# Late F2 with traded banks and a seeded sum, and a transposed key-value product in small array tiles

## The chip, the cores and the metric

The kernel runs on one NeuronCore of a Trainium2 chip. The metric is the device time of one execution in microseconds (us). The kernel before takes 149.12 us, the median of 7 runs, which lie between 149.07 and 150.18.

The engines are TensorE (PE, matmuls, with PEld for the loads of the stationary operand), VectorE (DVE), ScalarE (ACT), GpSimd (POOL) and SyncE (SP, which issues nearly all transfers). Matmuls write to PSUM, eight banks of 512 fp32 columns. ACT and DVE take results out of PSUM.

## What is computed

x has 2048 tokens of 448 features. It is normalised once and feeds two branches, whose sum is added to x:

```
xn = layernorm(x)
# branch A: linear attention, 16 heads of 28
q, k, v = split(xn @ wqkv)
phi(u) = concat(softmax(u @ w_phi), softmax(-(u @ w_phi)))      # 56 features a head
kv  = phi(k)^T @ v            # 56 x 28 for each head, over all tokens
z   = sum over tokens of phi(k)
o   = (phi(q) @ kv) / (phi(q) @ z + 1e-6)
A   = concat(o) @ wo
# branch B: dense, 448 -> 1792 -> 448
B   = silu(xn @ w1) @ w2
out = x + A + B
```

All inputs and the output are bf16; products are summed in fp32.

## The kernel before

Tokens are cut in 16 tiles of 128, and in 4 chunks of 512 (c = 0 to 3). All matmuls come in pairs (`pair`, line 439): one half of the pair contracts over partitions 0 to 63 (LO), the other over 64 to 127 (HI), and each writes a bank of its own. So every matmul uses 64 rows and 128 columns of the array, and a pair runs side by side. PSUM's banks form four slots of two: slots 0 to 2 rotate (`take`, `give`), slot 3 (banks 6 and 7) is fixed.

The units of work, in the order that PE runs them:

- Chunk 0 is transposed and sent through F1 in pieces. Here the two halves of a pair trade banks from one phase to the next (`F1ph`, line 663), and `swapped` (line 638) makes PE wait for its own last matmul on a bank before the other half writes there.
- `F1` (line 683): hT = silu(w1^T xn^T), 7 blocks for a chunk, 7 pairs of 512 columns each; ACT evicts 1024 columns.
- `QK` (line 693): phi of q and k for one tile, with exponentials on ACT, sums on DVE and products on POOL; the q half goes through a DMA transpose into phT.
- `V` (line 719): v of two tiles. Each head has 29 columns in `vb`: 28 of v and a column of ones, which gives z.
- `KV` (line 733): for one tile, 8 pairs of matmuls. The stationary operand is phi(k) of two heads (128 columns with padding), the moving one is v of the same two heads (58 columns). LO and HI tokens sum into banks 6 and 7 over all 16 tiles. Only the two diagonal blocks of each product are used.
- `KVZ_fin` (line 740): after the last KV, ACT copies one bank's diagonal blocks, DVE adds the other's; even heads end up on partitions 0 to 55, odd ones on 64 to 119 of KVZ.
- `F2` (line 749): one tile of hT^T w2, 14 pairs of 448 columns. The two halves are two partial sums of the same tile in two banks. For tiles 0 to 7 (`F2_early`) ACT and DVE add them into Ye and POOL adds x. For tiles 8 to 15 (`F2_late`, line 772), ACT copies one bank to Yl, POOL adds x to it, and the other bank stays for WO.
- `U` (line 784): phi(q) @ kv of two tiles, 16 pairs of 29 columns; then den, reciprocal and four products on DVE, and a DMA transpose into oT.
- `WO` (line 810): two tiles of o @ wo, 7 pairs of 448 columns, each half for a tile of its own. For early tiles it starts its banks; for late ones it goes on in the F2 banks. DVE adds Ye or Yl, writes x_sb, and SP stores two tiles.

Order: chunks 0 to 2 interleave F1, QK, V, KV and early F2. In chunk 3, phase_e comes before F1. KV of the last tile follows F1's block 4, KVZ_fin comes behind it, and the first U stands inside block 6. The late part (lines 1056 to 1064) goes over k = 0 to 3: U of a late pair, F2_late of its two tiles, WO of an early pair and WO of the late pair.

PE's order is the order of the program. For the other engines, `schedule` (line 203) plans: a list scheduler places each operation by its estimated start and its due time, tries several passes and then shaken due times (`shaken=60`), and keeps the order with the shortest planned span. A wait is a semaphore for each operation that depends on another engine, so what stands behind it on its engine waits too.

Of the kernel before, what the change touches and what calls it, by code (L numbers as in the profile page):

```python
# [7 lines left out]
F32 = mybir.dt.float32  # L8
# [132 lines left out]
class _Prog:  # L141
# [58 lines left out]
            return 230.0  # L200
        return 110.0

    def schedule(self, pe0, passes=6, shaken=60):
        ops = self.ops
        for o in ops:
            for d in o.deps:
                ops[d].users.append(o.id)
            for d in o.odeps:
                assert ops[d].eng == o.eng, "order-only deps must be same-engine"
                ops[d].users.append(o.id)  # L210
        t = 0.0
        when = {}
        seen = False
        for o in ops:
            if o.eng == "pe":
                if o.name != "warm" and not seen:
                    seen = True
                    t = max(t, pe0)
                when[o.id] = t
                t += o.dur  # L220
        best = None
        base = when
        for k in range(passes + shaken):
            if k == passes:
                base = {oid: best[2][oid][0] for oid in best[1]["pe"]}
            order, span = self._pass(base, k - passes + 1)
            if best is None or span < best[0]:
                best = (span, order, [(o.start, o.end) for o in ops])
                if k >= passes:
                    base = {oid: ops[oid].start for oid in order["pe"]}  # L230
            if k < passes:
                base = {oid: ops[oid].start for oid in order["pe"]}
        for o, (a, b) in zip(ops, best[2]):
            o.start, o.end = a, b
        self.order = best[1]
        self.makespan = best[0]
        return best[1]
# [92 lines left out]
def bass_parallel_sum__linear_kernel_hedgehog__dense_activation_silu__prompt_kernel(  # L330
# [21 lines left out]
    with es:  # L352
        def sb(name, shape, dt):
            return es.enter_context(nc.sbuf_tensor(name, shape, dt))

        NE, NV, NX, NXC, NYE, NYL, NH = 6, 3, 4, 3, 8, 4, 3
        x_sb = sb("x_sb", [128, NT, D], BF16)
        xT_all = sb("xT", [128, NXC * NS * 512], BF16)
        w1_sb = sb("w1_sb", [128, NS, FH * 128], BF16)
# [8 lines left out]
        xnd = sb("xnd", [128, NX, NS * 128], BF16)  # L368
        Ye = sb("Ye", [128, NYE, D], F32)
        KVZ = sb("KVZ", [128, 8, DH + 1], BF16)  # L370
        KVt = sb("KVt", [128, 8, DH + 1], F32)
        BD = sb("BD", [128, NB, 2 * DH], BF16)
        ident = sb("ident", [128, 128], BF16)
        neghalf = sb("neghalf", [128, 1], F32)
# [11 lines left out]
        phT = ph_all[:].rearrange("p (t c n) -> p t c n", t=NT, c=8)  # L386
        wsrc = hT[:, NH - 1, FT - 1, :]
        ones_bf = wsrc[:, 0:128]
        CH = NS * 512
        Yl = xT_all[:].bitcast(F32)[:, CH:CH + NYL * D].rearrange("p (y n) -> p y n", y=NYL)  # L390
        NO = 4
        E_all = E[:].rearrange("p a b n -> p (a b n)")
        o_pr = E_all[:, 8192:8192 + NO * NS * 128].rearrange("p (b n) -> p b n", b=NO)
# [11 lines left out]
        def bank(b):  # L405
            return psum[:, b * 512:(b + 1) * 512]
# [325 lines left out]

        def KV(t):
            P.unit = f"KV{t}"
            for c in range(8):
                pair([(bank(6 + q)[:, c * 58:(c + 1) * 58], E[HALF[q], t % NE, 1, c * 128:(c + 1) * 128],
                       vb[HALF[q], (t // 2) % NV, t % 2, c * 58:(c + 1) * 58], t == 0 and c == 0, t == NT - 1)
                      for q in range(2)], 58, "kv")

        def KVZ_fin():  # L740
            P.unit = "KVZ"
            for q, (p0, p1) in enumerate(((0, 56), (64, 120))):
                v = [bank(6 + b)[p0:p1, 0:464].rearrange("p (c n) -> p c n", n=58)[:, :, q * 29:(q + 1) * 29] for b in range(2)]
                tmp = KVt[p0:p1]
                act(tmp, v[0], ACTF.Identity, 232, name="kvz_a")
                dst = KVZ[p0:p1]
                dve(lambda e, dst=dst, a=v[1], tmp=tmp: e.tensor_tensor(dst, a, tmp, ALU.add), d_dve(232), [v[1], tmp], [dst], "kvz_d")

        def F2(t, mid=None, at=7):
            c, j = divmod(t, 4)  # L750
# [15 lines left out]
            give(sl)  # L766
            pool(lambda e: e.tensor_tensor(y, y, x_sb[:, t, :], ALU.add), 1110, [y, x_sb[:, t, :]], [y], "ye_x")  # L767

        ylc = [0]
        ysl = {}  # L770

        def F2_late(t, mid=None, at=7):
            sl = F2(t, mid, at)
            y = Yl[:, ylc[0] % NYL, :]
            ylc[0] += 1
            q = 1 - (t % 2)
            b = bank(2 * sl + q)[:, 0:D]
            act(y, b, ACTF.Identity, D, name="yl")
            pool(lambda e: e.tensor_tensor(y, y, x_sb[:, t, :], ALU.add), 1110, [y, x_sb[:, t, :]], [y], "yl_x")  # L779
            ysl[t] = (sl, y)  # L780

        uc = [0]

        def U(t, sl=3):
            P.unit = f"U{t}"
            for i, tt in enumerate((t, t + 1)):
                for c in range(8):
                    o0 = i * 232 + c * 29
                    pair([(bank(2 * sl + q)[:, o0:o0 + 29], phT[q * 64:q * 64 + 56, tt, c, :], KVZ[q * 64:q * 64 + 56, c, :], True, True)
                          for q in range(2)], 29, "u", dur=25.0)  # L790
            ub = uc[0] % NO
            uc[0] += 1
            Uv = two(sl)[:, :, 0:464].rearrange("p b (c n) -> p b c n", n=29)
            dn = den[:, ub, :].rearrange("p (b c) -> p b c", b=2)
            dve(lambda e: e.tensor_scalar(dn, Uv[:, :, :, DH], EPS_DEN, None, ALU.add), 200, [Uv], [den[:, ub, :]], "den")
            dve(lambda e: e.reciprocal(rden[:, ub, :], den[:, ub, :]), 360, [den[:, ub, :]], [rden[:, ub, :]], "rden")
            for i in range(2):
                for q in range(2):
                    src = bank(2 * sl + q)[:, i * 232:(i + 1) * 232].rearrange("p (c n) -> p c n", n=29)[:, :, 0:DH]
                    src = src.rearrange("p c (s e) -> p c s e", e=4)  # L800
                    r = rden[:, ub, q * 16 + i * 8:q * 16 + (i + 1) * 8]
                    rb = r[:, :, None, None].broadcast_to([128, 8, NS, 4])
                    dst = o_pr[:, ub].rearrange("p (s n) -> p s n", s=NS)[:, :, i * 64:(i + 1) * 64].rearrange("p s (c r e) -> p c r s e", r=2, e=4)[:, :, q]
                    dve(lambda e, dst=dst, src=src, rb=rb: e.tensor_tensor(dst, src, rb, ALU.mult), d_dve(224),  # L804
                        [src, r], [dst], "o")
            P.dma(lambda e: e.dma_start_transpose(out=oT[:, ub], in_=o_pr[:, ub]), 0, reads=[o_pr[:, ub]],
                  writes=[oT[:, ub]], name="oT_dma", issue=1250.0, fixed=3100.0)
            return ub

        def WO(t, ub, sl, parts=((0, D),)):  # L810
            P.unit = f"WO{t}"
            late = t in ysl
            if late:
                s0, y0 = ysl[t]
                s1, y1 = ysl[t + 1]
            else:
                s0 = s1 = sl
                y0, y1 = (Ye[:, tt % NYE, :] for tt in (t, t + 1))
            bks = (2 * s0, 2 * s1 + 1)
            for a, b in parts:  # L820
                for s in range(NS):
                    pair([(bank(bks[q])[:, a:b], oT[HALF[q], ub, s, :], wo_sb[HALF[q], s, a:b],
                           (not late) and s == 0, s == NS - 1) for q in range(2)], b - a, "wo")
                for q, y in enumerate((y0, y1)):
                    bk = bank(bks[q])[:, a:b]
                    dst = x_sb[:, t + q, a:b]
                    dve(lambda e, bk=bk, y=y[:, a:b], dst=dst: e.tensor_tensor(dst, bk, y, ALU.add), d_dve(b - a),  # L827
                        [bk, y[:, a:b]], [dst], "out")
                P.dma(lambda e, a=a, b=b: e.dma_start(out=ov[:, t:t + 2, a:b], in_=x_sb[:, t:t + 2, a:b]),
                      service(2 * 128 * (b - a) * 2, 2 * (b - a)), reads=[x_sb[:, t:t + 2, a:b]], name="out_dma", out_slot=True)  # L830
            give(s0)
            if s1 != s0:
                give(s1)

        def FT_tr(b2):
            P.unit = "FT"
# [190 lines left out]

        ub = {}

        def first_u():  # L1030
            ub[EPAIRS[0]] = U(EPAIRS[0])

        LATE = list(range(8, 16))
        EPAIRS = [0, 2, 4, 6]
        for c in range(NCH):
            if c == NCH - 1:
                phase_e(c, F2E[c])
            if c > 0:
                for i in range(FH):
                    F1(c, i, first_u if c == NCH - 1 and i == 6 else None)  # L1040
                    if i in ((3, 4, 5, 6) if c == 1 else (1, 2, 4, 5) if c == 2 else (1, 2, 3, 4)):
                        kv(1)
                    if c == NCH - 1 and i == 4:
                        KVZ_fin()
# [8 lines left out]
                give(sl)  # L1053
            ub[t] = U(t, sl)

        for k in range(4):
            l0, e = LATE[2 * k], EPAIRS[k]
            if k:
                nextu(l0)
            F2_late(l0, None if k else (lambda: nextu(LATE[0], None)), 3)  # L1060
            F2_late(l0 + 1, (lambda: nextu(EPAIRS[k + 1])) if k + 1 < 4 else None)
            sl = take()
            WO(e, ub[e], sl)
            WO(l0, ub[l0], None)

        order = P.schedule(5500.0)
        ops = P.ops
# [105 lines left out]
```

The softmax here doesn't subtract the row's maximum and nothing guards it: scores larger than these inputs give would overflow.

## Time and profile before

| what | value |
|---|---|
| median of 7 runs | 149.12 us |
| the profiled execution | 149.75 us |
| its span | 147.86 us |
| PE busy | 141.8 us, 96% of the span |
| DVE busy | 96.3 us, 65% |
| ACT busy | 85.5 us, 58% |
| POOL busy | 84.5 us, 57% |
| granted clock of TensorE | 1.00 |
| KV on PE, 256 matmuls | 6.1 us busy |
| late F2 to the last matmul | 109.36 to 144.2 us |

Busy time counts the length of each instruction; matmuls overlap, and the length of each holds a modelled tail. What one costs in a full stream is read from the distance of the starts instead. The span runs from the first to the last instruction of the trace; the time of an execution has 1.89 us more around it.

### The profile page before, as it was taken

The numbers are of one execution on the slowest core, as the hardware profiler recorded it, in microseconds if no ns is written. First come the engines' busy times: TensorE is split into PE (matmuls) and PEld (weight loads), VectorE is DVE, ScalarE is ACT, GpSimd is POOL, SyncE is SP. The second block draws the span as 40 slices with busy tenths as digits, with TensorE's granted clock in tenths as the row PEclk, the third lists the DMA queues.
The fourth block names the chain that finished last, engine by engine and source line by source line (L and its number), as shares of the span: only waits on it lengthen the run. The fifth ranks groups of instructions, "written<-read, shape, count | busy, mean of one in ns | idle before, by whom it ended". The sixth has DMA issues, their size and how long they took to land.

```text
span 147.9 us, 4912 instructions
## 1 busy us (share of the span) xinstructions
PE 141.8 (96%) x2118; PEld 86.9 (59%) x2118; DVE 96.3 (65%) x182; ACT 85.5 (58%) x109; POOL 84.5 (57%) x95
## 2 busy tenths in 40 slices
PE   6999999999999999999999999999999999999990
PEld 2589875555555555555555556655566566666550
DVE  1867369999996496841067997871154884848533
ACT  4247779988667794975987758598571111011110
POOL 3335024149999959899122999999972204122230
PEclk9999999999999999999999999999999999999999
DMA  4998989964919982379760092333779244853323
GB/s 128 389 235 197 304 248 262 112 137 124 202 25 103 191 165 69 93 159 138 155 136 0 0 110 36 71 75 73 41 176 94 51 112 124 119 140 72 104 72 124
DMA packets 43709, 19.10 MB, mean 129 GB/s; under 512 B 36712, under 2 KB 43048, under 8 KB 43688
## 3 DMA queue, kind: packets, MB, share of 16 engines
q1 hardware_dynamic: 43032, 17.87, 60.5%
q10 hardware_dynamic: 656, 0.92, 1.8%
q8 instruction: 16, 0.26, 0.9%
q14 instruction: 5, 0.04, 0.1%
HBM read 8.17 MB, written 1.84 MB: 68 GB/s over the span
## 4 chain that ended last, share of the span: by engine, by line
PE 93%; DVE 2%; DMA 2%; issue 1%; DVEq 0%; ACT 0%
PE psum L448 92%; DMA x_sb<-in_A_x_dram 2%; PE psum L461 1%; DVE st L575 1%; DVE x_sb L827 0%; DVEq L1124 0%; DVE mv L579 0%; DVE ve L581 0%; ACT xT L466 0%; DVE xnd L598 0%; DVEq L1113 0%
## 5 line engine op out<-in xcount | busy, mean ns | idle before, releaser
L715 POOL TENSOR_TENSOR E<-E,Rk 128x896 bf16<-128x896 bf16 x32 | 53.3, 1698 | 7.1 <-DVE Rk L710 5.1
L448 PE MATMUL psum<-xT,w_sb 64*128 64x512 bf16 (+2 forms) x522 | 46.9, 323 | 0.2
L448 PE MATMUL psum<-w_sb,hT 64*128 64x448 bf16 x448 | 45.2, 349 | 0.0
L448 PEld LDWEIGHTS psum<-w_sb,hT 64*128 64x128 bf16 x448 | 24.1, 94 | 16.6
L708 DVE TENSOR_REDUCE Sk<-E 128x64 f32<-128x1792 bf16 x16 | 31.9, 2004 | 2.9 <-ACT E L466 2.9
L466 ACT ACTIVATE hT<-psum 128x1024 bf16<-128x1024 f32 (+1 forms) x29 | 28.0, 993 | 9.8 <-PE psum L448 9.6
L448 PEld LDWEIGHTS psum<-xT,w_sb 64*128 64x128 bf16 x522 | 25.2, 94 | 13.8 <-issue 0.4
L466 ACT ACTIVATE E<-psum 128x896 bf16<-128x896 f32 x32 | 27.4, 917 | 6.4 <-PE psum L448 5.2
L466 ACT ACTIVATE xT<-psum 128x448 f32<-128x448 f32 (+3 forms) x14 | 6.6, 475 | 31.7 <-PE psum L448 27.8
L448 PE MATMUL psum<-wqk,xT 64*128 64x448 bf16 x224 | 23.7, 349 | 0.0
L779 POOL TENSOR_TENSOR xT<-xT,x_sb 128x448 f32<-128x448 f32 x8 | 8.3, 1032 | 25.0 <-ACT xT L466 21.6
L448 PEld LDWEIGHTS psum<-wqk,xT 64*128 64x128 bf16 x224 | 12.2, 94 | 8.6
L583 POOL TENSOR_TENSOR rstd<-ve,neghalf 128x1 f32<-128x1 f32 x16 | 9.1, 570 | 7.4 <-DVE ve L581 6.6
L767 POOL TENSOR_TENSOR Ye<-Ye,x_sb 128x448 f32<-128x448 f32 x8 | 8.2, 1036 | 8.9 <-DVE Ye L765 8.9
L575 DVE BATCH_NORM_STATS2 st<-x_sb 128x6 f32<-128x448 bf16 x16 | 9.6, 603 | 3.9 <-DMA x_sb<-in_A_x_dram 3.9
L591 DVE TENSOR_SCALAR xnd<-x_sb,mv,rstd 128x896 bf16<-128x896 bf16 x12 | 8.3, 722 | 5.8 <-POOL rstd L583 5.7
L448 PE MATMUL psum<-wv_sb,xT 64*128 64x448 bf16 x112 | 12.0, 349 | 0.0
L765 DVE TENSOR_TENSOR Ye<-psum,Ye 128x448 f32<-128x448 f32 x8 | 5.0, 621 | 10.3 <-ACT Ye L466 10.3
L448 PE MATMUL psum<-wo_sb,E 64*128 64x448 bf16 x112 | 11.3, 349 | 0.0
L804 DVE TENSOR_TENSOR E<-psum,rden 128x224 bf16<-128x224 f32 x32 | 10.3, 383 | 0.4
L448 PEld LDWEIGHTS psum<-wo_sb,E 64*128 64x128 bf16 x112 | 6.2, 94 | 4.4
L448 PEld LDWEIGHTS psum<-wv_sb,xT 64*128 64x128 bf16 x112 | 5.9, 94 | 4.0
(47 smaller groups left out, 102.4 us busy)
## 6 DMA issues: line engine op xcount, KB each, us to landing
w_sb<-in_B_w_dram SPq DMA_DIRECT2D x4, 448.0 KB, 5.5
out_dram<-x_sb SPq DMA_DIRECT2D x8, 224.0 KB, 2.2
w_sb<-in_B_w_dram SPq DMA_DIRECT2D x4, 336.0 KB, 5.6
x_sb<-in_A_x_dram SPq DMA_DIRECT2D x2, 448.0 KB, 4.6
wv_sb<-in_A_wqkv_dram SPq DMA_DIRECT2D x2, 392.0 KB, 5.0
wo_sb<-in_A_wo_dram SPq DMA_DIRECT2D x14, 56.0 KB, 2.3
phT<-in_A_wqkv_dram SPq DMA_DIRECT2D x3, 224.0 KB, 3.5
w_sb<-in_B_w_dram ACTq DMA_DIRECT2D x1, 448.0 KB, 5.1
```

The source lines that it names most:

```text
L448: ins = e.matmul(dst, lhsT, rhs, start=st, stop=sp, skip_group_check=True)
L461: ins = e.transpose(dst, src, idn)
L466: return P.op("act", d_act(n), lambda e: e.activation(dst, src, func, scale=scale), reads=reads or [src], writes=writes or [dst], table=ta ...
L575: P.op("dve", 630, lambda e: e.bn_stats(st6[:, t, :], xs), [xs], [st6[:, t, :]], name="bnst", ordered=od)
L583: P.op("pool", 580, lambda e: e.tensor_tensor(rstd[:, t:t + 1], ve[:, t:t + 1], neghalf[:], ALU.pow), [ve[:, t:t + 1], neghalf[:]], [rstd[ ...
L591: dve(lambda e: e.tensor_scalar(dst, src, mv[:, t, 0:1], rstd[:, t:t + 1], ALU.subtract, ALU.mult), 734, [src, mv[:, t, 0:1], rstd[:, t:t ...
L708: dve(lambda e: e.tensor_reduce(Sk[:, t % 3, :].rearrange("p (h g) -> p h g", g=2), Er, AXL.X, ALU.add), d_dve(1792), [Er], [Sk[:, t % 3, ...
L715: pool(lambda e, Eh=Eh, Rb=Rb: e.tensor_tensor(Eh, Eh, Rb, ALU.mult), 1770, [Eh, Rh], [Eh], "phi%d" % qk)
L765: dve(lambda e: e.tensor_tensor(y, b, y, ALU.add), d_dve(D), [b, y], [y], "ye_d")
L767: pool(lambda e: e.tensor_tensor(y, y, x_sb[:, t, :], ALU.add), 1110, [y, x_sb[:, t, :]], [y], "ye_x")
L779: pool(lambda e: e.tensor_tensor(y, y, x_sb[:, t, :], ALU.add), 1110, [y, x_sb[:, t, :]], [y], "yl_x")
L804: dve(lambda e, dst=dst, src=src, rb=rb: e.tensor_tensor(dst, src, rb, ALU.mult), d_dve(224), [src, r], [dst], "o")
```

## The change

It has two parts.

1. Late F2 works on two tiles at once. In a first phase (`F2_ph(.., 0, ..)`) the LO half of the contraction goes to the first tile's bank and the HI half to the second tile's. In a second phase (1) the halves trade banks, so that each bank ends up with one tile's full sum. Before the first phase ACT writes x into both banks (`seed`), and no matmul clears them, so x is part of the sum, and WO of the pair goes on in the same banks. Nothing is left to add: ACT copies both banks to x_sb. Yl and POOL's additions are gone. U and WO are put between the phases. The last pair (14 and 15) is cut into column halves of 224, each in a slot of its own, with F2, WO, eviction (ACT for one bank, DVE for the other) and store by halves.
2. KV is transposed. v of one head (29 columns) is the stationary operand and phi(k) of the same head (64 columns) the moving one. Four heads share a bank on partitions 0, 32, 64 and 96, so that a matmul uses 64 rows and 32 columns of the array, and eight different tiles of the array follow one another. Only products of matching heads are made: 32 matmuls of 64 columns for a token tile, where 16 of 58 stood. At the end ACT and DVE add the two banks to KVb (in the space of xnd), two pairs of PE transposes (`KVZ_tr`) turn it, and ACT and DVE evict KVZ. KVZ_tr takes the first U's place inside F1's last block, and the first U moves into F2 of tile 8.

The first U matmul alone clears its bank now, and the planner shakes 160 times.

```diff
         def KV(t):
             P.unit = f"KV{t}"
-            for c in range(8):
-                pair([(bank(6 + q)[:, c * 58:(c + 1) * 58], E[HALF[q], t % NE, 1, c * 128:(c + 1) * 128],
-                       vb[HALF[q], (t // 2) % NV, t % 2, c * 58:(c + 1) * 58], t == 0 and c == 0, t == NT - 1)
-                      for q in range(2)], 58, "kv")
+            for a in range(4):
+                mms = []
+                for j in range(4):
+                    h = 2 * ((j // 2) * 4 + (a // 2) * 2 + j % 2) + a % 2
+                    for q in range(2):
+                        mms.append((bank(6 + q)[32 * j:32 * j + 29, a * 64:(a + 1) * 64],
+                                    vb[HALF[q], (t // 2) % NV, t % 2, h * 29:(h + 1) * 29],
+                                    E[HALF[q], t % NE, 1, h * 64:(h + 1) * 64], t == 0 and a == 0, t == NT - 1))
+                pair(mms, 64, "kv", dur=40.0)
...
+            v = [bank(6 + b)[:, 0:256] for b in range(2)]
+            act(KVt[:], v[0], ACTF.Identity, 256, name="kvz_a")
+            dve(lambda e: e.tensor_tensor(KVb, v[1], KVt[:], ALU.add), d_dve(256), [v[1], KVt[:]], [KVb], "kvz_d")
+
+        def KVZ_tr():
+            P.unit = "KVZ"
+            for b in range(2):
+                tpair([(bank16(6 + q)[:, b * 64:(b + 1) * 64], KVb[HALF[q], b * 128:(b + 1) * 128], ident[HALF[q], q * 64:(q + 1) * 64])
+                       for q in range(2)], 64, "kvz_tr")
...
+        def seed(t, sl, a, b):
+            P.unit = f"F2_{t}"
+            xs = [x_sb[:, t + q, a:b] for q in range(2)]
+            bk = [bank(2 * sl + q)[:, a:b] for q in range(2)]
+            for q in range(2):
+                act(bk[q], xs[q], ACTF.Identity, b - a, name="seed")
+
+        def F2_ph(t, sl, ph, a, b, mid={}):
+            c, j = divmod(t, 4)
+            for ft in range(FT):
+                P.unit = f"F2_{t + ph}"
+                mms = []
+                for q in range(2):
+                    h = q ^ ph
+                    mms.append((bank(2 * sl + h)[:, a:b], hT[HALF[q], c % NH, ft, (j + h) * 128:(j + h + 1) * 128],
+                                w2_sb[HALF[q], ft, a:b], False, False))
+                swapped(pair(mms, b - a, "f2"), (2 * sl, 2 * sl + 1), ph)
+                if ft in mid:
+                    mid[ft]()
...
+        def WO_two(t, ub, sl, a, b):
+            WO_mm(t, ub, sl, a, b, True)
+            for q in range(2):
+                bk = bank(2 * sl + q)[:, a:b]
+                dst = x_sb[:, t + q, a:b]
+                if q and b - a < D:
+                    dve(lambda e, bk=bk, dst=dst: e.tensor_copy(dst, bk), d_dve(b - a), [bk], [dst], "out")
+                else:
+                    act(dst, bk, ACTF.Identity, b - a, name="out")
+            store(t, a, b)
+            give(sl)
...
-                    F1(c, i, first_u if c == NCH - 1 and i == 6 else None)
+                    F1(c, i, KVZ_tr if c == NCH - 1 and i == 6 else None)
...
+        def ph0(l, a, b, mid={}):
+            sls[l, a] = take()
+            seed(l, sls[l, a], a, b)
+            F2_ph(l, sls[l, a], 0, a, b, mid)
+
+        def ph1(l, a, b):
+            F2_ph(l, sls[l, a], 1, a, b)
+
+        def wo2(e, l):
+            WO(e, ub[e])
+            nextu(l + 2)
+            WO_two(l, ub[l], sls[l, 0], 0, D)
+
+        M = D // 2
+        ph0(8, 0, D, {1: lambda: nextu(0), 4: lambda: nextu(8, None)})
+        nextu(2)
+        ph1(8, 0, D)
+        ph0(10, 0, D)
+        wo2(0, 8)
+        ph1(10, 0, D)
+        nextu(4)
+        ph0(12, 0, D)
+        wo2(2, 10)
+        ph1(12, 0, D)
+        nextu(6)
+        ph0(14, 0, M)
+        wo2(4, 12)
+        ph1(14, 0, M)
+        ph0(14, M, D)
+        WO(6, ub[6])
+        ph1(14, M, D)
+        WO_two(14, ub[14], sls[14, 0], 0, M)
+        WO_two(14, ub[14], sls[14, M], M, D)
```

More of the change, by code (lines that the diff above doesn't have):

```diff
@@ L201, in lat, with schedule @@
         return 110.0
-    def schedule(self, pe0, passes=6, shaken=60):
+    def schedule(self, pe0, passes=6, shaken=160):
         ops = self.ops
@@ L354, in sb @@
             return es.enter_context(nc.sbuf_tensor(name, shape, dt))
-        NE, NV, NX, NXC, NYE, NYL, NH = 6, 3, 4, 3, 8, 4, 3
+        NE, NV, NX, NXC, NYE, NH = 6, 3, 4, 3, 8, 3
         x_sb = sb("x_sb", [128, NT, D], BF16)
@@ L370, in bass_parallel_sum__linear_kernel_hedgehog__dense_activation_silu__prompt_kernel @@
         KVZ = sb("KVZ", [128, 8, DH + 1], BF16)
-        KVt = sb("KVt", [128, 8, DH + 1], F32)
+        KVt = sb("KVt", [128, 256], F32)
+        KVb = xnd[:, 0, 0:256]
         BD = sb("BD", [128, NB, 2 * DH], BF16)
@@ L388, in bass_parallel_sum__linear_kernel_hedgehog__dense_activation_silu__prompt_kernel @@
         ones_bf = wsrc[:, 0:128]
-        CH = NS * 512
-        Yl = xT_all[:].bitcast(F32)[:, CH:CH + NYL * D].rearrange("p (y n) -> p y n", y=NYL)
         NO = 4
@@ L734, in KV @@
             P.unit = f"KV{t}"
-            for c in range(8):
-                pair([(bank(6 + q)[:, c * 58:(c + 1) * 58], E[HALF[q], t % NE, 1, c * 128:(c + 1) * 128],
-                       vb[HALF[q], (t // 2) % NV, t % 2, c * 58:(c + 1) * 58], t == 0 and c == 0, t == NT - 1)
-                      for q in range(2)], 58, "kv")
+            for a in range(4):
[7 more added lines that the diff above has]
+                pair(mms, 64, "kv", dur=40.0)
         def KVZ_fin():
             P.unit = "KVZ"
[L742 to L747, printed above, removed]
+            v = [bank(6 + b)[:, 0:256] for b in range(2)]
[7 more added lines that the diff above has]
+            for q in range(2):
+                src = bank16(6 + q)[:, 0:128].rearrange("p (c n) -> p c n", n=32)[:, :, 0:29]
+                dst = KVZ[:, 4 * q:4 * q + 4, :]
+                if q:
+                    dve(lambda e, dst=dst, src=src: e.tensor_copy(dst, src), d_dve(116), [src], [dst], "kvz_e")
+                else:
+                    act(dst, src, ACTF.Identity, 116, name="kvz_e")
         def F2(t, mid=None, at=7):
@@ L767, in F2_early @@
             pool(lambda e: e.tensor_tensor(y, y, x_sb[:, t, :], ALU.add), 1110, [y, x_sb[:, t, :]], [y], "ye_x")
[L769 to L780, printed above, removed]
+        def seed(t, sl, a, b):
[16 more added lines that the diff above has]
+                    mid[ft]()
         uc = [0]
@@ L788, in U @@
                     o0 = i * 232 + c * 29
-                    pair([(bank(2 * sl + q)[:, o0:o0 + 29], phT[q * 64:q * 64 + 56, tt, c, :], KVZ[q * 64:q * 64 + 56, c, :], True, True)
+                    pair([(bank(2 * sl + q)[:, o0:o0 + 29], phT[q * 64:q * 64 + 56, tt, c, :], KVZ[q * 64:q * 64 + 56, c, :], i == 0 and c == 0, True)
                           for q in range(2)], 29, "u", dur=25.0)
@@ L808, in U, with store, WO_mm @@
             return ub
-        def WO(t, ub, sl, parts=((0, D),)):
+        def store(t, a, b):
+            P.dma(lambda e: e.dma_start(out=ov[:, t:t + 2, a:b], in_=x_sb[:, t:t + 2, a:b]),
+                  service(2 * 128 * (b - a) * 2, 2 * (b - a)), reads=[x_sb[:, t:t + 2, a:b]], name="out_dma", out_slot=True)
+        def WO_mm(t, ub, sl, a, b, seeded):
             P.unit = f"WO{t}"
[L812 to L833, printed above, removed]
@@ new lines, in WO_mm, with WO @@
+            for s in range(NS):
+                op = pair([(bank(2 * sl + q)[:, a:b], oT[HALF[q], ub, s, :], wo_sb[HALF[q], s, a:b], (not seeded) and s == 0, s == NS - 1)
+                           for q in range(2)], b - a, "wo")
+                swapped(op, (2 * sl, 2 * sl + 1), 0)
+        def WO(t, ub):
+            sl = take()
+            WO_mm(t, ub, sl, 0, D, False)
+            for q in range(2):
+                bk = bank(2 * sl + q)[:, 0:D]
+                y = Ye[:, (t + q) % NYE, :]
+                dst = x_sb[:, t + q, :]
+                dve(lambda e, bk=bk, y=y, dst=dst: e.tensor_tensor(dst, bk, y, ALU.add), d_dve(D), [bk, y], [dst], "out")
+            store(t, 0, D)
+            give(sl)
@@ L835, in FT_tr @@
+        def WO_two(t, ub, sl, a, b):
+            WO_mm(t, ub, sl, a, b, True)
+            for q in range(2):
+                bk = bank(2 * sl + q)[:, a:b]
+                dst = x_sb[:, t + q, a:b]
+                if q and b - a < D:
+                    dve(lambda e, bk=bk, dst=dst: e.tensor_copy(dst, bk), d_dve(b - a), [bk], [dst], "out")
+                else:
+                    act(dst, bk, ACTF.Identity, b - a, name="out")
+            store(t, a, b)
+            give(sl)
         def FT_tr(b2):
@@ L1028, in bass_parallel_sum__linear_kernel_hedgehog__dense_activation_silu__prompt_kernel @@
         ub = {}
-        def first_u():
-            ub[EPAIRS[0]] = U(EPAIRS[0])
         LATE = list(range(8, 16))
@@ L1054, in nextu @@
             ub[t] = U(t, sl)
[L1056 to L1064, printed above, removed]
+        sls = {}
+        def ph0(l, a, b, mid={}):
[28 more added lines that the diff above has]
+        WO_two(14, ub[14], sls[14, M], M, D)
         order = P.schedule(5500.0)
```

## The prediction

> **What bounds the kernel now.** I read the page first, then busy time by stage, the chain, the timeline of the switch from F1 to late F2, the timeline of the end, and groups kept apart by shape. The page's first part:
>
> ```profile
> PE 141.8 (96%) x2118; PEld 86.9 (59%) x2118; DVE 96.3 (65%) x182; ACT 85.5 (58%) x109; POOL 84.5 (57%) x95
> ```
>
> By stage (busy us of PE, PEld, DVE, ACT and POOL, then clock and DMA):
>
> ```profile
> 33.87:97.47 63.60, 63.60 (x810) 36.78 (x808) 44.90 (x58) 47.73 (x56) 52.43 (x47) 1.00 0.62 107
> 97.47:109.36 11.89, 11.89 (x196) 6.69 (x194) 4.12 (x7) 9.09 (x12) 11.89 (x9) 1.00 0.54 82
> 109.36:144.20 34.84, 34.80 (x562) 21.37 (x558) 21.97 (x60) 5.37 (x9) 8.89 (x9) 1.00 0.48 98
> 144.20:147.90 3.70, 0.00 (x0) 0.00 (x0) 1.16 (x2) 0.00 (x0) 0.00 (x0) 0.99 0.33 124
> ```
>
> PE is full in every stage up to 144.2 us, at full clock, and the chain (start, length, what) says the same:
>
> ```profile
> 20.48 123.70 PE psum L448 x1724
> 144.18 0.03 issue
> 144.20 0.02 DVEq L1113
> 144.22 0.04 issue
> 144.27 0.62 DVE x_sb L827
> 144.89 0.53 DVEq L1124
> ```
>
> So only two things move the time: what PE has to stream, with any new hole in it, and the 3.7 us after its last matmul. Work taken off ACT, DVE or POOL before 144.2 is worth nothing by itself. The end in the timeline:
>
> ```profile
> 141.34 2.82 PE L448 MATMUL psum<-wo_sb,E 64*128 64x448 bf16 x28
> 144.27 1.16 DVE L827 TENSOR_TENSOR x_sb<-psum,xT 128x448 bf16<-128x448 f32 x2 [0.24 <-PE psum L448]
> ```
>
> For small matmuls, the starts of neighbouring PE rows give the price (a row's own length includes about 0.16 us of modelled tail: 349 ns against 187 ns of streaming for 448 columns):
>
> ```profile
> 105.71 0.40 PE L448 MATMUL psum<-vb,E 64*128 64x58 bf16 x16
> 105.94 1.90 PE L448 MATMUL psum<-xT,w_sb 64*128 64x512 bf16 x16
> 107.66 0.57 PE L448 MATMUL psum<-KVZ,phT 56*128 56x29 bf16 x32
> 108.07 0.39 PE L448 MATMUL psum<-xT,w_sb 64*128 64x512 bf16 x2
> ```
>
> One token tile's KV takes 0.23 us (8 pairs, 29 ns a pair); one U takes 0.41 us (16 pairs, 25.6 ns a pair). Every tile shape in the trace is 64 rows by 128 columns.
>
> **The change, part by part.**
>
> *KV.* Per token tile, 16 matmuls of 58 columns become 32 of 64 columns, in four groups of eight; a group fills eight array tiles of 64x32. The lower bound of a group is the streaming of 64 columns: the 14 transposes of 64 columns at 11.25 us take 0.20 us, 29 ns a pair, so 4 x 29 = 0.117 us. The upper bound is U's sustained rate, 12.8 ns a matmul with its weight load: 32 x 12.8 = 0.41 us. Between them: two weight loads of 94 ns each finish within 0.10 us at 8.67 us (row below), so instructions for different tiles can start about 5 ns apart; eight give 40 ns a group, 0.16 us a tile. I take this, because both U's and KV's rates are those of one tile used again, and here eight are in turn. Against 0.23 that is 16 x 0.07 = -1.12 us (bounds -1.81 and +2.88).
>
> *Change of tile shape.* KV stands in 14 blocks between 128-column matmuls (12 of one token tile, two of two), so there are 28 changes of shape. The trace has none. Below, changes of the moving length, of the operation and of 64 to 56 rows cost nothing to see. Above, the nearest is PE waiting for its own results and starting again, in chunk 0:
>
> ```profile
> 8.67 0.10 PEld L448 LDWEIGHTS psum<-xT,w_sb 64*128 64x128 bf16 x2
> 8.96 0.14 PEld L448 LDWEIGHTS psum<-xT,w_sb 64*128 64x128 bf16 x4 [0.20 <-issue]
> ```
>
> That hole is 0.20 us; 28 of them are 5.6 us. I take nothing, as every change that the trace does have is free; the upper end is the first rival.
>
> [...]
>
> *Turning KVZ.* Two pairs of 64-column transposes are added on PE: 0.06 us. Of ACT and DVE, two half-size evictions each become one of 256 columns (about 0.4 us by the 0.36 to 0.40 us rows of 232) and one of 116. Cover: KV ends at 105.94; ACT starts its copy at 106.27, ends at 106.7, DVE's sum ends near 107.1; the turn comes on PE after F1's 1.51 us and one pair, 107.67. ACT then has a silu (1.02 us), two seeds (0.54 each) and its half of the eviction, until about 109.1; U(0) comes at 105.94 + 3.08 + 0.38 = 109.4. Cost nothing, with 0.3 us of cover; without it, the lateness itself.
>
> *Late F2.* A pair of tiles still has 28 pairs of matmuls, so PE's work is the same; in chunk 0 traded banks at 256 columns run at the same 109 ns a pair as the untraded. ACT loses 8 copies (0.543 us) and gets 6 seeds and 6 evictions of 448 columns and 6 pieces of 224 (0.365): 8.7 us in place of 4.3, in a stage of 34.8. POOL's 8 adds (1.03 us) go, as do 8 of DVE's 16 adds (0.62). None was on the chain. New waits of PE: (a) F2_ph(8) on its seeds, 108.8 against 109.0; (b) the right half of 14 on seeds that follow DVE's two adds of WO(4): DVE ends about 2.0 us after WO(4), ACT 0.4 later or up to 2.9 where it does an eviction first, PE arrives after 0.41 + 1.32 + 1.34 = 3.07; (c) each phase change on PE's own last use of the bank: at least a U (0.41 us) or half a WO (0.67) lies between, against a tail of 0.16. (d) WO(14) on its transpose: DVE needs 0.47 + 0.19 + 0.35 + 0.62 + 1.28 = 3.0 us after U(14), the transpose lands 2.7 later, and PE comes after 6.7. What is queued behind a wait on PE is everything; I cost all at nothing. On SP, transposes now stand behind stores that wait for ACT (U(10)'s behind store 8), but have over 5 us to spare.
>
> *Column halves.* 28 pairs of F2 and 7 of WO are each cut in two. From 109 ns at 256 columns and 189 at 448, 224 columns cost 96, so 2 x 96 - 189 = 2 to 3 ns a pair: 35 pairs, +0.08 us.
>
> *The end.* Before: two DVE adds after one another, 1.16 us (groups by shape: 620 ns each). After: 224 columns on ACT and 224 on DVE, side by side:
>
> ```profile
> L872 DVE CAST wqk<-psum 128x224 bf16<-128x224 f32 x1 | 0.4, 381 | 0.0
> L466 ACT ACTIVATE wqk<-psum 128x224 bf16<-128x224 f32 x1 | 0.4, 365 | 0.0
> ```
>
> 0.38 us: -0.78 us. The last store has half the bytes in runs of 448 in place of 1792; stores landed in 1.9 to 4.2 us, median 2.2, with most of it not bytes, so I take no change, with bounds of -0.3 and +2.0; the 4.2 was not the last store's, which ends 2.4 us after DVE. SP's issue of the left half's store (0.5 us) ends before the right half is ready (0.67 later).
>
> *Sum.* -1.12 + 0 + 0.06 + 0 + 0.08 - 0.78 = -1.76 us. The span of 147.86 becomes 146.1; the profiled execution's 149.75 becomes 147.99. That execution lies 0.63 above the median of 149.12, so the forecast is 149.12 - 1.76 = 147.36.
>
> **The rivals.**
>
> First, the other side: changes of tile shape drain PE. Place: both edges of 14 KV blocks. From 63 ns each (1.76/28) the gain is gone; from 90 ns it is slower by over 0.5%; at 100 ns, half of the hole above, 147.36 + 2.8 = 150.2; at the full 0.20, 153.0. For it: nothing shows that such a change is free, and weights for the other shape may not load ahead. Against: all other changes are free.
>
> Second: issue binds KV. At U's 12.8 ns a matmul it costs +2.88 in place of -1.12: 151.4. For it: U never goes faster. Against: U's 25.6 ns a pair is close to KV's 29 for twice the columns, which looks like a floor of one tile.
>
> Third: the transposed KV streams no faster than before (0.23 us) and the rest holds: 148.5.
>
> Fourth: the late stage stalls, most of all WO(14) on a transpose that lands after 4.1 us (the slowest here) rather than 2.7: 0.5 us later, 147.9.
>
> **How the numbers follow.** About 0.5% (0.75 us) is what a measurement here tells from no change: under 148.37 is faster, over 149.87 slower. The forecast with the fourth rival has 0.56; the first rival 0.28, of which 0.02 (holes under 36 ns) is faster, 0.06 (36 to 90 ns) the same and 0.20 slower; the second 0.08; the third 0.08, the same. That makes faster 0.58, same 0.14, slower 0.28. The likeliest case's own range is 146.4 (KV at 0.117 us, store 0.3 better: -1.81 + 0.14 - 1.08) to 148.2. The range for all goes up to 151.0, which leaves out the second rival and drains over 0.13 us.
>
> **What would show it.** KV blocks of 0.16 us a tile between starts, and no hole at their edges: a hole of 0.1 us on each side is the first rival, an even 0.4 us block the second. PE's idle time in the late stage near 0; one eviction of 0.38 us on ACT and DVE after the last matmul, near 143.2, and a span near 146.1. The prediction fails if the edges of KV cost over 63 ns, or KV takes over 0.27 us a tile (0.16 + 1.76/16).

## The result, and the profile after

The changed kernel takes 150.82 us (median of 13 runs) against 149.39 for the kernel before, measured beside it: a ratio of 1.0102 with a 95% interval of 1.0083 to 1.0121, some 1.5 us slower. The forecast was 147.36, faster, with a range up to 151.0. The time lies inside the range, but on the other side. The profiled execution took 151.29 us with a span of 149.6. Ratios here leave out executions over 1.5% above the fastest of their kernel.

The stages of the changed kernel (busy us of PE, PEld, DVE, ACT and POOL, then clock, DMA share and GB/s): the middle, late F2, and what follows the last matmul.

```profile
34.15:97.41 63.26, 63.26 (x924) 31.00 (x920) 43.98 (x57) 46.24 (x54) 51.35 (x46) 1.00 0.58 104
111.49:146.80 35.31, 35.27 (x664) 22.78 (x660) 19.15 (x57) 8.36 (x17) 0.17 (x1) 1.00 0.42 102
146.80:149.60 2.80, 0.00 (x0) 0.00 (x0) 0.39 (x1) 0.36 (x1) 0.00 (x0) 1.00 0.29 85
```

The end is shorter, as forecast: 2.8 us in place of 3.7. The last matmul ends 2.6 us later. Busy time hides where: PE shows as busy for 63.26 us of 63.26, as it did before, because each matmul's length holds a modelled tail of 0.16 us, and a hole shorter than that lies under it. Only the distance of the starts shows it. KV between blocks of F1, before:

```profile
41.65 0.40 PE L448 MATMUL psum<-vb,E 64*128 64x58 bf16 x16
41.88 1.68 PE L448 MATMUL psum<-xT,w_sb 64*128 64x512 bf16 x14
43.39 0.40 PE L448 MATMUL psum<-vb,E 64*128 64x58 bf16 x16
```

and after:

```profile
42.16 0.31 PE L447 MATMUL psum<-E,vb 64*29 64x64 bf16 x32
42.41 1.68 PE L447 MATMUL psum<-xT,w_sb 64*128 64x512 bf16 x14
44.02 0.31 PE L447 MATMUL psum<-E,vb 64*29 64x64 bf16 x32
```

Before, KV holds its place for 0.23 us and the 14 matmuls of F1 for 1.51. After, it is 0.25 us and 1.61, although nothing in F1 changed. A round of KV and F1 is 1.86 us in place of 1.74.

The weight loads show what happens at the edge. Before, KV's first load starts 0.22 us ahead of its first matmul, while F1 still streams. After, no load starts before the matmul that it belongs to. Before, and then after:

```profile
41.43 0.50 PEld L448 LDWEIGHTS psum<-vb,E 64*128 64x128 bf16 x16
42.16 0.19 PEld L447 LDWEIGHTS psum<-E,vb 64*29 64x29 bf16 x32 [0.42 <-issue]
```

So F1's last matmuls run out before anything of KV begins: by the single starts of the trace, KV begins 0.09 us later than another pair of F1 would have. What PE waits for there can't be told from this trace. With two token tiles in one block it is worse. Before, and then after:

```profile
88.62 1.50 PE L448 MATMUL psum<-wv_sb,xT 64*128 64x448 bf16 x14
89.94 0.63 PE L448 MATMUL psum<-vb,E 64*128 64x58 bf16 x32
90.40 0.54 PE L448 MATMUL psum<-wqk,xT 64*128 64x448 bf16 x3
```

```profile
89.89 1.49 PE L447 MATMUL psum<-wv_sb,xT 64*128 64x448 bf16 x14
91.31 0.77 PE L447 MATMUL psum<-E,vb 64*29 64x64 bf16 x64
92.01 0.55 PE L447 MATMUL psum<-wqk,xT 64*128 64x448 bf16 x4
```

V and the double KV take 1.78 us before and 2.12 after. The sum over the whole kernel: 12 single blocks at +0.12, 1.5 us; two double ones at +0.35, 0.7; the turn of KVZ and the column halves 0.14; the end -0.9. That is +1.44 us, against +1.5 measured. The profiles agree: from the first QK matmul to the end of the last matmul it is 120.89 us before and 123.20 after, +2.31, and with the end +1.41. Another 0.28 us of this profile's span lies ahead of the first QK matmul (23.56 us against 23.27), in code that both kernels share. Over the profiles of this case that point lies anywhere from 22.5 to 24.2 us, so it belongs to the execution and not to the change.

### The profile page after: what moved, and what is told of

It is laid out like the page before. It is cut to its first block, busy times and chain, and to the rows that moved or that the text cites. A ratio compares the mean times of both kernels' runs of the same rounds, so it can differ in the third digit from the quotient of the medians.

```text
span 149.6 us, 5571 instructions
## 1 busy us (share of the span) xinstructions
PE 144.5 (97%) x2448; PEld 82.5 (55%) x2448; DVE 91.9 (61%) x176; ACT 88.9 (59%) x119; POOL 76.2 (51%) x87
## 4 chain that ended last, share of the span: by engine, by line
PE 92%; DMA 5%; ACTq 1%; issue 0%; ACT 0%; DVE 0%
PE psum L447 90%; DMA w_sb<-in_B_w_dram 5%; PE psum L460 1%; ACTq L478 1%; ACT L515 0%; DVE x_sb L859 0%; ACT tabw L515 0%
## 5 line engine op out<-in xcount | busy, mean ns | idle before, releaser
L447 PE MATMUL psum<-w_sb,hT 64*128 64x448 bf16 (+1 forms) x504 | 45.4, 328 | 0.0
L447 PEld LDWEIGHTS psum<-xT,w_sb 64*128 64x128 bf16 x522 | 23.7, 94 | 15.7 <-DMA w_sb<-in_B_w_dram 0.6
L465 ACT ACTIVATE psum<-x_sb 128x448 f32<-128x448 bf16 (+1 forms) x10 | 4.6, 468 | 20.2 <-PE psum L447 19.6
L447 PEld LDWEIGHTS psum<-wqk,xT 64*128 64x128 bf16 x224 | 11.1, 94 | 9.7
L447 PE MATMUL psum<-wo_sb,E 64*128 64x448 bf16 (+1 forms) x126 | 11.9, 328 | 0.0
L849 DVE TENSOR_TENSOR x_sb<-psum,Ye 128x448 bf16<-128x448 f32 x8 | 4.8, 606 | 9.0 <-PE psum L447 6.2
L709 DVE RECIPROCAL Rk<-Sk 128x64 f32<-128x64 f32 x16 | 8.2, 532 | 0.1
L465 ACT ACTIVATE vb<-psum 128x896 bf16<-128x896 f32 x8 | 7.4, 924 | 0.9 <-PE psum L447 0.8
```

The source lines that it names most:

```text
L447: ins = e.matmul(dst, lhsT, rhs, start=st, stop=sp, skip_group_check=True)
L465: return P.op("act", d_act(n), lambda e: e.activation(dst, src, func, scale=scale), reads=reads or [src], writes=writes or [dst], table=ta ...
L709: dve(lambda e: e.reciprocal(Rk[:, t % 3, :], Sk[:, t % 3, :]), 64 * 6.25 + 155, [Sk[:, t % 3, :]], [Rk[:, t % 3, :]], "Rk")
L849: dve(lambda e, bk=bk, y=y, dst=dst: e.tensor_tensor(dst, bk, y, ALU.add), d_dve(D), [bk, y], [dst], "out")
```

## The experiments

Theory after the result: part 2 (KV) loses 2.2 us by changes of tile shape and by its double blocks, and part 1 (late F2) gains at the end. The rival: the late stage loses, and KV is harmless.

### Each part alone

Late F2 without the new KV, and the new KV without late F2 (its first U moved as in the changed kernel). In the first, KV and KVZ_fin are those of before and KVZ_tr is left out.

> Part 1 of the change alone: late F2 with traded banks, seeds and the last pair in halves; KV as before. Theory (all of the loss is in KV): PE's stream grows by 0.08 us for the halves, the end behind the last matmul is 0.86 us shorter as in the changed kernel, so about 0.7 to 0.8 us less than before, a ratio of 0.995. Rival (the late stage has holes of its own, from seeds or traded banks): ratio 1.000 or more, with idle time on PE between 109 and 146 us.

Measured: a ratio of 0.9994 (0.9966 to 1.0023). No loss, but not the gain either: the expected 0.995 lies outside the interval, and the rival's idle time is there. What ate the gain stands further down.

In the second, KV, KVZ_fin and KVZ_tr are those of the change, F2_late and WO those of before (code cut to the moved U):

```diff
-            F2_late(l0, None if k else (lambda: nextu(LATE[0], None)), 3)
+            F2_late(l0, None if k else {1: lambda: nextu(EPAIRS[0]), 4: lambda: nextu(LATE[0], None)})
```

> Part 2 alone: transposed KV in 64x32 tiles with the turn at the end, late F2 as before. Theory: 12 single blocks cost 0.35 us where 0.23 stood, two double ones 0.81 where 0.46 stood, and the turn 0.06: +2.2 us, a ratio of 1.015, with the end as long as before (3.7 us). Rival (KV costs nothing and the late part is what loses): ratio 0.995.

Measured: 1.0149 (1.0113 to 1.0185), where 1.015 was expected. The whole loss is in part 2.

### More changes of shape, the same matmuls

```diff
-        def KV(t):
+        def KV(t, parts=range(4)):
...
-            for a in range(4):
+            for a in parts:
...
-                        kv(1)
+                        t = pend.pop(0)
+                        F1(c, i, lambda: KV(t, range(2)), 3)
+                        KV(t, range(2, 4))
```

> The changed kernel with each of the 12 single KV blocks cut in two halves, the first inside F1's block after its fourth pair, the second behind it: the same matmuls, 24 more changes of tile shape. Theory (each change costs PE 0.1 us, whatever is in the block): 12 x 0.2 = +2.4 us over the changed kernel, a ratio to before of 1.026. Rival (PE is held by the rate at which KV's instructions are issued): no more than the changed kernel, 1.010, or a little less, since shorter blocks fit the queue better.

Measured: 1.0267 (1.0233 to 1.0301); 1.026 was expected if a change of shape costs 0.1 us. The timeline of PE in this run:

```profile
43.22 0.25 PE L447 MATMUL psum<-E,vb 64*29 64x64 bf16 x16
43.41 0.82 PE L447 MATMUL psum<-xT,w_sb 64*128 64x512 bf16 x6
44.16 0.25 PE L447 MATMUL psum<-E,vb 64*29 64x64 bf16 x16
```

Half a KV block still takes 0.185 us to the next start, and 6 matmuls of F1 take 0.75 where the rate of before (1.51 us for 14) makes 0.65. So one block costs 0.10 us ahead of it, and 0.185 + 0.10 for 16 matmuls against 0.246 + 0.106 for 32. The difference, 0.061 to 0.067 us for 16 matmuls, is some 4 ns each, and what is left, 0.23 us, is paid once for a block, for 16 matmuls as for 32. A semaphore does not explain the edge: KV's first load waits on one before the change too, where the edge is missing, and in the second half of a split block it waits on none and the edge is there.

### Fewer changes of shape, longer blocks

```diff
-                    if i in ((3, 4, 5, 6) if c == 1 else (1, 2, 4, 5) if c == 2 else (1, 2, 3, 4)):
-                        kv(1)
+                    if i == (6 if c == 1 else 5 if c == 2 else 4):
+                        kv(4)
```

> The changed kernel with the 12 single blocks merged to three of four tiles each: the same matmuls, 18 fewer changes of tile shape. Theory A (only the changes of shape cost, 0.13 us of streaming for each tile): 9 x 0.2 = -1.8 us against the changed kernel, a ratio to before of 0.998. Theory B (a block beyond the first 32 matmuls is held by issue at 0.46 us a tile, as the second half of the double blocks): three blocks of 0.35 + 3 x 0.46 = 1.73 us in place of 4 x 0.35 = 1.41, so +1.0 us against the changed kernel, a ratio of 1.016.

Measured: 1.0149 (1.0114 to 1.0185): theory B. Its timeline:

```profile
44.47 1.51 PE L447 MATMUL psum<-E,vb 64*29 64x64 bf16 x128
45.92 0.55 PE L447 MATMUL psum<-wqk,xT 64*128 64x448 bf16 x4
```

128 matmuls take 1.45 us. The first 32 of a block cost 0.25 with the way out, so the further ones cost (1.45 - 0.25) / 3 = 0.40 us for each 32, and 0.46 in the double blocks (0.706 - 0.246), against 0.12 for the first 32. The single starts of both traces show why the two numbers differ: in every block of over one tile the 33rd matmul starts 0.10 us after the 32nd, once, and from there each 32 take 0.37 us, 11.6 ns a matmul. What KV saves by fewer edges it loses to this hole and this rate; from the first QK matmul to the end of the last one, this run takes 0.50 us longer than the changed kernel, half of what theory B had. Why the first 32 go faster than the later ones is not shown, and theory B's cause, issue, was not tested. The hole always stands where the second token tile begins, so it is open, too, whether the count of 32 makes it.

### Other shapes

KV in tiles of 64 rows by 64 columns, two heads to a matmul. The turn of KVZ is not fitted to it, so KVZ ends up with other products, and the run serves for its times alone (code cut to the new matmuls):

```diff
...
+                for j in range(2):
+                    c = 2 * a + j
+                    for q in range(2):
+                        mms.append((bank(6 + q)[64 * j:64 * j + 58, a * 128:(a + 1) * 128],
+                                    vb[HALF[q], (t // 2) % NV, t % 2, c * 58:(c + 1) * 58],
+                                    E[HALF[q], t % NE, 1, c * 128:(c + 1) * 128], t == 0 and a == 0, t == NT - 1))
...
```

> The changed kernel with KV in tiles of 64x64: v of two heads (58 columns) stationary, phi(k) of the two (128 columns) moving, 16 matmuls for a token tile; the turn at the end is left as it is, so KVZ holds other products than the reference's. Theory (the hole belongs to the change of shape): edges of 0.23 us a block as in 64x32 tiles, and 4 x 0.055 = 0.22 us of streaming: 0.45 us for a single block in place of 0.35, and 0.68 for a double one in place of 0.81, so +0.9 us over the changed kernel, ratio 1.016. Rival (the hole belongs to 32-column tiles): 0.22 to 0.25 us a block, ratio 0.997.

Measured: 1.0130 (1.0065 to 1.0196). The timeline answers the question better than the time does:

```profile
42.44 0.42 PE L447 MATMUL psum<-E,vb 64*58 64x128 bf16 x16
42.78 1.69 PE L447 MATMUL psum<-xT,w_sb 64*128 64x512 bf16 x14
44.40 0.42 PE L447 MATMUL psum<-E,vb 64*58 64x128 bf16 x16
```

KV holds 0.35 us and F1 1.61, 0.10 too long again: 0.45 us for the block, as expected. If 0.22 of it is streaming, an estimate from the kernel before (109 ns a pair of 256 columns, so 0.055 us for 128), 0.23 is left for the two edges; by the single starts, 0.09 us stand at each. So the edge does not belong to 32 columns. From the first QK matmul to the end of the last one this run takes 0.96 us longer than the changed kernel, where 0.9 was expected.

Late F2 over 128 rows, on top of late F2 alone, where only the rows change:

```diff
-                for q in range(2):
-                    h = q ^ ph
-                    mms.append((bank(2 * sl + h)[:, a:b], hT[HALF[q], c % NH, ft, (j + h) * 128:(j + h + 1) * 128],
-                                w2_sb[HALF[q], ft, a:b], False, False))
+                mms = [(bank(2 * sl + ph)[:, a:b], hT[:, c % NH, ft, (j + ph) * 128:(j + ph + 1) * 128],
+                        w2_sb[:, ft, a:b], False, False)]
...
```

> Late F2 alone, with F2's late matmuls over all 128 rows: one phase for each tile, 14 matmuls of 448 columns, no traded halves; U and WO stay at 64 rows. 20 changes of shape, all in rows. Theory (any change of tile shape costs PE about 0.115 us): +2.3 us over late F2 alone, a ratio of 1.014, with holes of about 0.1 us at each edge of F2. Rival (the cost belongs to narrow column tiles alone, by their weight loads): no holes, ratio 0.999.

Measured: 1.0043 (1.0008 to 1.0079), less than the theory's 1.014 and more than the rival's 0.999. The timeline:

```profile
109.95 0.55 PE L446 MATMUL psum<-w_sb,hT 128*128 128x448 bf16 x2
110.44 0.57 PE L446 MATMUL psum<-KVZ,phT 56*128 56x29 bf16 x32
110.94 0.74 PE L446 MATMUL psum<-w_sb,hT 128*128 128x448 bf16 x3
111.61 0.57 PE L446 MATMUL psum<-KVZ,phT 56*128 56x29 bf16 x32
```

Two matmuls of 448 columns hold 0.49 us in place of 2 x 0.189, and a U 0.50 in place of 0.41: 0.11 and 0.09 us at the edges, now between 64 and 128 rows. From the first late F2 matmul to the end of the last matmul it takes 37.2 us, against 35.8 with late F2 alone, of which 0.52 is a hole that this run does not have: 1.9 us for 20 changes, 0.1 each. On the clock of the whole kernel less of that arrived, some 0.5% over late F2 alone. Late F2 alone has the hole of the next section in it, which this run does not; whether that makes the whole difference is not shown.

### Where late F2's gain goes

With late F2 alone the end is 0.9 us shorter, and yet no time is won. Its timeline around the last pair (PE's WO(14) is the last line; SPq is the issue of transfers):

```profile
136.88 0.34 SPq L816 DMA_DIRECT2D out_dram<-x_sb  x1
138.11 1.23 SPq L811 DMA_TRANSPOSE E<-E  x1
140.65 1.51 PE L446 MATMUL psum<-w_sb,hT 64*128 64x224 bf16 x28
142.51 1.52 PE L446 MATMUL psum<-wo_sb,E 64*128 64x224 bf16 x28 [0.35 <-DMA E<-E]
```

The 28 matmuls of 224 columns stream for 1.34 us, so WO(14) should start at 141.99. It starts at 142.51, when U(14)'s transpose lands, 4.4 us after its issue. The same transpose landed after 2.6 us in the kernel before. So there is a hole of 0.52 us, and the runs scatter from 148.6 to 151.3. Not all of that scatter has to be the transpose's, since the point of the first QK matmul alone moved by 1.7 us between profiles.

The next run gives the planner that landing time for this one transpose:

```diff
-                  writes=[oT[:, ub]], name="oT_dma", issue=1250.0, fixed=3100.0)
+                  writes=[oT[:, ub]], name="oT_dma", issue=1250.0, fixed=4400.0 if t == 14 else 3100.0)
```

> Late F2 alone, with one number of the planner changed: the transpose of U(14) is said to land after 4.4 us in place of 3.1. The planner then puts U(14)'s products on DVE ahead of the second add of WO(4), and the store of that pair behind the transpose. Theory (late F2's gain of 0.86 us at the end is eaten by the wait for this transpose): it is issued 0.6 us earlier, no hole of PE ahead of WO(14), a ratio of 0.993 to 0.996. Rival (the hole is not what holds late F2 back): ratio 0.999 as with late F2 alone.

Measured: 0.9993 (0.9970 to 1.0016), the rival's number, though the hole went as the theory asked. The transpose, which now has that store behind it, landed after 2.7 us; the hole ahead of WO(14) is gone, and another has come:

```profile
136.66 1.28 DVE L809 TENSOR_TENSOR E<-psum,rden 128x224 bf16<-128x224 f32 x4
137.86 0.61 DVE L833 TENSOR_TENSOR x_sb<-psum,Ye 128x448 bf16<-128x448 f32 x1
138.51 0.36 ACT L464 ACTIVATE psum<-x_sb 128x224 f32<-128x224 bf16 x1 [0.51 <-DVE x_sb L833]
138.93 0.27 PE L446 MATMUL psum<-w_sb,hT 64*128 64x224 bf16 x2 [0.59 <-ACT psum L464]
```

U(14)'s products now run ahead of WO(4)'s second add on DVE. The bank of that add is the one that the right half of tiles 14 and 15 is seeded in, so the seed waits for the add, and PE for the seed: 0.78 us from start to start. Both chains hang on the same DVE at the same time; the halves of the last pair give either one or the other too little room. The two holes account for the times of PE: from the first QK matmul to the end of the last one, late F2 alone takes 0.61 us longer than the kernel before and this run 0.85, which is 0.52 and 0.78 and the 0.08 of the column halves. The runs now lie between 148.9 and 149.9, without the scatter.

Two runs have the last pair in full width, which needs no second slot and so no seed behind WO(4). ACT evicts one bank and DVE the other:

```diff
-                if q and b - a < D:
+                if q and t == 14:
...
-        ph0(14, 0, M)
+        ph0(14, 0, D)
         wo2(4, 12)
-        ph1(14, 0, M)
-        ph0(14, M, D)
+        ph1(14, 0, D)
         WO(6, ub[6])
-        ph1(14, M, D)
-        WO_two(14, ub[14], sls[14, 0], 0, M)
-        WO_two(14, ub[14], sls[14, M], M, D)
+        WO_two(14, ub[14], sls[14, 0], 0, D)
```

> Late F2 alone, with the last pair in full width (ACT evicts one bank, DVE the other) in place of halves: PE streams 0.08 us less, the last eviction takes 0.6 us in place of 0.39, and from the end of U(14) to WO(14) there are 1.32 + 2.65 + 1.32 = 5.3 us in place of 6.7. Theory (WO(14) waits for U(14)'s transpose, issued 2.8 us after U(14) and landing 2.6 to 4.4 later): a hole of 0.1 to 1.9 us ahead of WO(14), 0.2 to 1.5 us longer than late F2 in halves, a ratio of 1.001 to 1.009. Rival (the transpose is there in time): 0.15 us longer, ratio 1.000.

The times lie in two groups of six, 148.4 to 149.2 and 150.6 to 151.4, with a granted clock of 0.99 to 1.00 in both. Measured: 0.9961 (0.9926 to 0.9996), which is the first group alone; the median of all 12 is 149.92, against 149.49 for the kernel before. The profiled execution is of the first group. It has no hole, but no room either: its transpose landed after 2.7 us, and the first weight load of WO(14) still waited 0.19 us for it.

```profile
142.13 1.14 PEld L446 LDWEIGHTS psum<-wo_sb,E 64*128 64x128 bf16 x14 [0.19 <-DMA E<-E]
```

Neither theory had it so: the planner puts U(14)'s products ahead of the second add here, which the expectation left out. The second runs U(14) ahead of WO(4):

```diff
         ph0(14, 0, D)
-        wo2(4, 12)
+        nextu(14)
+        WO(4, ub[4])
+        WO_two(12, ub[12], sls[12, 0], 0, D)
```

> Late F2 alone with the last pair in full width, and U(14) moved ahead of WO(4), so that its transpose has 1.3 us more before WO(14) and DVE takes U(14)'s products before the adds of WO(4); no seed hangs on those adds here. Theory (what late F2 loses is the wait for this transpose, which lands after 2.6 us in some executions and 4.4 in others): no hole ahead of WO(14) or elsewhere, runs within 1 us of each other, 0.5 us less than before from the shorter end, a ratio of 0.995 to 0.997. Rival (the executions 2 us longer with late F2 in full width have another cause): the same two groups of times, 148.4 to 149.2 and 150.6 to 151.4.

Measured: 0.9977 (0.9958 to 0.9996), and one group, 148.35 to 149.47. The second group is gone when U(14) comes earlier. That is what the theory asks for, though no profile of an execution of the second group exists that would show its hole, so the cause of that group is argued and not shown. Behind the last matmul:

```profile
144.46:147.60 3.14, 0.00 (x0) 0.00 (x0) 0.62 (x1) 0.54 (x1) 0.00 (x0) 0.99 0.40 146
```

The end is 3.14 us in place of 3.7, and that is the whole gain in the profile, as PE takes 120.88 us from the first QK matmul to the end of the last one, and 120.89 before. Late F2 with the old KV beats the kernel before by 0.2%, and the changed kernel by 1.2%. What makes the transpose late is open. A store stands 1.2 us ahead of U(14)'s transpose on SP's queue in the four profiles where it took 3.6 to 4.4 us (the changed kernel, the two runs with split and merged KV blocks, late F2 alone), and where that store stands elsewhere it took 2.6 to 2.7; but a transpose earlier in the kernel before took 4.0 us as well with its last store 3 us ahead.

## Why the prediction was wrong

**KV's streaming: right, and even better.** 0.16 us a tile was taken; by the difference between blocks of 16 and 32, the first 32 matmuls of a block cost 0.12, nearly the lower bound of 0.117. By the single starts it is 0.15, with 0.09 at each edge; the 0.03 between the two counts is counted with the edges here. Starts of 4 ns apart on different tiles hold. The weight loads overlap as well: one of 29 columns shows 88 ns, and the 32 of a block 0.19 us together. The unknown price was placed well between its ends for those tiles, and the second rival (0.41 us by issue) is wrong for them. Its price fits what comes behind 32 matmuls, 0.37 us and a hole of 0.10, in two of the 16 tiles; its cause was not tested.

**The change of shape: the step that failed.** "I take nothing, as every change that the trace does have is free" is the sentence that cost the forecast. None of those changes touches the tile shape, so they were no rows for it; the only near row was the other bound, a hole of 0.20 us. The runs show 0.23 us for each block, in and out together, or 0.115 us for a change: 28 x 0.115 = 3.2 us. With that alone in place of nothing, the forecast would have been 147.36 + 3.2 = 150.6, against 150.82. That this comes so close has some luck in it, as the faster first tiles (14 x -0.04) and the slower second ones (2 x +0.30) cancel. The first rival named the place, the price (150.2 at 0.1 us) and the point from which it decides (63 ns). It was given 0.28.

**KV in all**, by these terms: 14 first tiles at 0.12 for 0.23 (-1.5), two second tiles at 0.46 for 0.23 (+0.5), edges +3.2: +2.2 us where -1.12 was forecast.

**The turn and the halves: right.** Four transposes take 0.06 us between their neighbours' starts, and PE waits for nothing around them or in the late stage. 28 matmuls of 224 columns take 1.338 us, 96 ns a pair.

**The end: right, mis-sized a little.** -0.78 was forecast, -0.9 came: the eviction takes 0.39 us as forecast, and the half store lands after 1.8 us, where the last store before took 1.9, which was in the bounds.

**The waits of late F2: right for the changed kernel, and by luck.** It has no hole in the late stage; its last transpose landed after 3.6 us, 0.3 ahead of need, where the landing of this transpose went up to 4.4. In the run without the new KV the fourth rival came true, with 4.4 us and 0.52 of hole. (The terms listed under (d) add up to 2.9 us and not 3.0, and with its own numbers the fourth rival is 0.4 us and not 0.5; nothing hangs on either.) Both waits named as (b) and (d) were the right two; what was missed is that they compete for DVE, so that easing one makes the other.

## What to carry to other kernels

Do not mix tile shapes of TensorE in a full stream for small gains: every change that was tried, in rows or in columns, cost 0.1 us each way here, so a block in another shape has to save more than 0.2 us by itself. Where the trace has no row for what a change introduces, the bound that is nearest in kind counts, not the number of other things that are free. And a shorter end only pays if the last chain (here U, DVE, transpose, WO) has room for the slowest landing of its transfer (4.4 us here for U(14)'s transpose), not the usual one (2.6 to 2.7).

## What the runs showed of the hardware

- A change of tile shape cost PE 0.09 to 0.12 us each way in these runs: 64x128 to 64x32, to 64x64, and to 128x128. PE's busy and idle times do not show it, since the modelled tails of the matmuls (0.16 us) cover it; the weight loads of the changed kernel do, as none of KV's starts before the change (idle for 0.42 us ahead of KV).
- Matmuls on eight tiles of 64x32 streamed at 4 ns each (0.061 us for 16) up to the 32nd of a block. Ahead of the 33rd, in the double blocks and those of four tiles, stands a hole of 0.10 us, and from there each took 11.6 ns on average. Why is not shown.
- The landing of U(14)'s transpose took 2.6 to 4.4 us in the profiles of the kernels here. With the last pair in full width, where it had 0.1 us to spare in the profile, 6 of 12 executions were 2 us longer; that the transpose makes them so is not shown.
